# Memory attention and SwiGLU on one core: the first pair's attention taken batch by batch, its root moved ahead of the transposes, PSUM banks named by a table

## The chip, the cores and the metric

The kernel runs on one core of one Trainium2 chip. The metric is device time in microseconds, from one launch that has all inputs in HBM and leaves the output there. Lower is better.

## What is computed

Eight batches of attention with 8 heads, 576 positions, head width 64 and 32 memory slots, and then one RMS-normed SwiGLU layer over the 4608 rows (width 512, inner width 1536), all in float32:

```python
a = softmax(phi, axis=seq)                      # (b, h, 576, 32)
k_m, v_m = a^T @ k, a^T @ v                     # (b, h, 32, 64) each
attn = softmax(q @ k_m^T / 8, axis=slots)       # (b, h, 576, 32)
x = (attn @ v_m) as rows of 512                 # (4608, 512)
xn = x / sqrt(mean(x*x) + 1e-6) * rms_g
out = (silu(xn @ w_gate) * (xn @ w_val)) @ w_out
```

## The kernel before

The batches go in four pairs. For a pair, phi's softmax numerators `e_bd` are multiplied with k and v (`kvp`, line 461), scaled by their sums (`si`, `im`, then `kb` and `vb`, lines 480 to 496) and transposed (`kvt`, copied to `km` and `vt`). Queries are scored against `km`, and a softmax over the 32 slots follows. The product with v_m is never written out for the SwiGLU layer. The scores `at` are scaled by the row's root and split into a high and a low part (`ath`, `atl`), v_m is multiplied into the weight columns (`vp`, `xh` and `xl`), and the gate and value products `pg` and `pv` (line 1069) take those two. The only use of `xp` (scores times v_m, line 845) is its sum of squares, from which the root `rinv` comes (lines 866 to 891). After silu and product, `po` (line 1126) multiplies with w_out and `acc` collects over the inner width. Weights come as float32, are split by bit arithmetic (lines 944 to 989) and are written back to DRAM for the later pairs.

The first pair has its own code, because nothing can hide its beginning. Its queries are loaded into `qs`, a tile for two slices of heads that holds batch 0 in the even and batch 1 in the odd partitions (`load_q`, line 545), so each of the four slices `s` is reordered (`qr`), transposed (`qtp`, copied to `qT`), scored and softmaxed for both batches at once (`q_steps`, `score_steps`). The normed scores stand in `first`. `x_steps(0)` transposes them (`tp`, line 747), copies them to `at`, makes `xp` and the root, and then multiplies `first` with a diagonal matrix of the root (`diag`, line 803, on ScalarE, and `ts`, line 811, on TensorE), so that the transposed and scaled scores come out in one matmul; `ath` (line 830, ScalarE) and `atl` (line 826, VectorE) split them.

The order of all work is written out: `parts` is a list of some 2,790 small steps, and `ISSUE` a table of numbers that says in which order they are put into the program. Each engine runs its own instructions in that order, and so does the SP queue, which issues every DMA. PSUM has two double tiles (`banks`) and four single ones (`bank`), which are handed out in turn:

```python
    def bank(name, shape=None):
        return ps.tile(shape or [P, 512], F32, tag="b", name=name, bufs=4)
```

Of the kernel before, what the change touches and what calls it, by code (L numbers as in the profile page):

```python
# [1230 lines left out]
```

## Time and profile before

| | |
|---|---|
| median of 3 runs | 792.76 us (792.66 to 794.98) |
| the profiled execution | 792.07 us |
| its span, first to last instruction | 790.3 us |
| TensorE (PE) busy | 748.9 us, 95% |
| VectorE (DVE) busy | 471.8 us, 60% |
| ScalarE (ACT) busy | 350.9 us, 44% |
| GpSimd (POOL) busy | 244.4 us, 31% |
| moved by DMA | 112.86 MB |
| mean granted TensorE clock | 0.991 |

Engine times are a union of the spans of its instructions; a share over the whole span mixes a beginning with little matmul work with a long stretch in which TensorE is never free. Idle time of an engine in the tables carries the name of what released it. The profiled execution has 1.8 us outside its span.

### The profile page before, as it was taken

The numbers are of one execution on the slowest core, as the hardware profiler recorded it, in microseconds if no ns is written. First come the engines' busy times: TensorE is split into PE (matmuls) and PEld (weight loads), VectorE is DVE, ScalarE is ACT, GpSimd is POOL, SyncE is SP. The second block draws the span as 40 slices with busy tenths as digits, with TensorE's granted clock in tenths as the row PEclk, the third lists the DMA queues.
The fourth block names the chain that finished last, engine by engine and source line by source line (L and its number), as shares of the span: only waits on it lengthen the run. The fifth ranks groups of instructions, "written<-read, shape, count | busy, mean of one in ns | idle before, by whom it ended". The sixth has DMA issues, their size and how long they took to land.

```text
span 790.3 us, 18128 instructions
## 1 busy us (share of the span) xinstructions
PE 748.9 (95%) x7496; PEld 639.0 (81%) x7496; DVE 471.8 (60%) x956; ACT 350.9 (44%) x697; POOL 244.4 (31%) x209
## 2 busy tenths in 40 slices
PE   4777988999999999999999999899999999999998
PEld 2565766788887988888888888788888888888886
DVE  6698878888776676465565374655454422444443
ACT  1668767665555544532354334442432335232221
POOL 0244555354432223322433212221232212121212
PEclk9799999999999999999999999999999999999999
DMA  9947775856583652253153654222241334112113
GB/s 331 375 148 214 200 184 198 275 177 213 196 216 85 198 152 95 80 174 98 67 181 123 153 170 99 86 81 71 92 134 54 117 110 147 53 56 80 54 54 120
DMA packets 111722, 112.86 MB, mean 143 GB/s; under 512 B 61460, under 2 KB 77848, under 8 KB 111640
## 3 DMA queue, kind: packets, MB, share of 16 engines
q1 hardware_dynamic: 111640, 111.70, 45.2%
q8 instruction: 59, 0.97, 0.5%
q14 instruction: 23, 0.19, 0.1%
HBM read 89.66 MB, written 22.02 MB: 141 GB/s over the span
## 4 chain that ended last, share of the span: by engine, by line
PE 81%; DVE 6%; ACT 5%; DMA 4%; SPq 2%; issue 1%; POOL 0%; ACTq 0%; DVEq 0%
PE po L1126 36%; PE pg L1069 17%; PE pv L1069 17%; PE vp L1034 5%; PE xp L845 2%; SPq L645 2%; DMA kvs<-in_k_dram 1%; PE kvp L461 1%; DMA qs<-in_q_dram 1%; PE S L670 1%; ACT wex L944 1%; DVE phi L407 1%; ACT xh L1051 1%; DMA raw<-in_moe_w_out_dram 1%; ACT L1080 1%
## 5 line engine op out<-in xcount | busy, mean ns | idle before, releaser
L1100 POOL TENSOR_TENSOR hl<-hf,hh 128x512 fp32r<-128x512 f32 (+1 forms) x84 | 120.0, 1431 | 311.8 <-ACT hh L1095 297.9
L1085 DVE TENSOR_TENSOR hf<-pv,sg 128x256 f32<-128x256 f32 (+1 forms) x192 | 85.5, 452 | 153.1 <-PE pv L1069 110.1
L1126 PE MATMUL po<-oh,hh 128*128 128x512 f32 x432 | 172.2, 399 | 2.3 <-ACT acc L1135 1.4
L1080 ACT ACTIVATE sg<-pg 128x256 f32<-128x256 f32 (+1 forms) x192 | 77.6, 411 | 213.9 <-PE pg L1069 183.3
L1137 DVE TENSOR_TENSOR acc<-po,acc 128x512 f32<-128x512 f32 x180 | 121.0, 685 | 84.5 <-PE po L1126 84.0
L1126 PE MATMUL po<-oh,hl 128*128 128x512 f32 x432 | 170.2, 394 | 0.0
L1126 PE MATMUL po<-ol,hh 128*128 128x512 f32 x432 | 169.2, 392 | 0.0
L1095 ACT CAST hh<-hf 128x512 fp32r<-128x512 f32 (+1 forms) x96 | 64.5, 675 | 86.5 <-DVE hf L1085 86.2
L1126 PEld LDWEIGHTS po<-oh,hh 128*128 128x128 f32 x432 | 81.1, 188 | 21.8 <-ACT acc L1135 2.2
L1126 PEld LDWEIGHTS po<-oh,hl 128*128 128x128 f32 x432 | 81.2, 188 | 17.9
L1126 PEld LDWEIGHTS po<-ol,hh 128*128 128x128 f32 x432 | 81.2, 188 | 13.5
L1069 PE MATMUL pv<-ath,xh 128*128 128x320 f32 (+1 forms) x384 | 84.6, 301 | 4.3 <-ACT sg L1080 3.3
L1069 PE MATMUL pg<-ath,xh 128*128 128x256 f32 (+1 forms) x384 | 85.8, 305 | 2.4 <-DVE hf L1085 1.4
L1069 PE MATMUL pv<-ath,xl 128*128 128x320 f32 (+1 forms) x384 | 81.4, 293 | 0.0
L1069 PE MATMUL pg<-ath,xl 128*128 128x256 f32 (+1 forms) x384 | 81.3, 293 | 0.0
L1069 PE MATMUL pg<-atl,xh 128*128 128x256 f32 (+1 forms) x384 | 81.3, 293 | 0.0
L1069 PE MATMUL pv<-atl,xh 128*128 128x320 f32 (+1 forms) x384 | 81.3, 293 | 0.0
L1049 DVE TENSOR_TENSOR xl<-vp,xh 128x512 fp32r<-128x512 f32 x96 | 64.3, 682 | 28.0 <-ACT xh L1051 27.8
L1069 PEld LDWEIGHTS pg<-ath,xh 128*128 128x128 f32 x384 | 62.7, 188 | 16.7 <-issue 5.0
L1069 PEld LDWEIGHTS pv<-ath,xh 128*128 128x128 f32 x384 | 63.4, 188 | 15.3 <-ACT sg L1080 5.3
L1051 ACT CAST xh<-vp 128x512 fp32r<-128x512 f32 x96 | 54.3, 590 | 29.8 <-PE pv L1069 11.7
L1069 PEld LDWEIGHTS pv<-atl,xh 128*128 128x128 f32 x384 | 61.3, 188 | 0.0
(121 smaller groups left out, 998.0 us busy)
## 6 DMA issues: line engine op xcount, KB each, us to landing
wc<-wd SPq DMA_DIRECT2D x36, 512.0 KB, 5.5
oh<-od SPq DMA_DIRECT2D x36, 256.0 KB, 3.6
ol<-od SPq DMA_DIRECT2D x36, 256.0 KB, 3.9
out_dram<-acc SPq DMA_DIRECT2D x36, 256.0 KB, 2.2
q<-in_q_dram SPq DMA_DIRECT2D x96, 72.0 KB, 2.9
raw<-in_moe_w_val_dram SPq DMA_DIRECT2D x12, 512.0 KB, 4.7
raw<-in_moe_w_gate_dram SPq DMA_DIRECT2D x12, 512.0 KB, 4.5
raw<-in_moe_w_out_dram SPq DMA_DIRECT2D x12, 512.0 KB, 4.7
```

Source lines behind the costliest of these rows:

```text
L645: load(d["q", cc][32 * g:32 * g + 32, s], q[b, 4 * cc + 2 * s + h].rearrange("(r x) d -> r x d", r=32)[:, :, 32 * half:32 * half + 32],)
L845: nc.tensor.matmul(xp[64 * j:64 * j + 64, s, t - t0, P * cc:P * cc + P], st["at", pr][rows, t, cc, 64 * j:64 * j + 64], st["kb", 2 * pr + ...
L1034: nc.tensor.matmul(vp[32 * g:32 * g + 32, flip(b, cc), cc, :], vm[pr][rows, b, hp, 32 * (g % 2):32 * (g % 2) + 32], w[rows, hp, :], start= ...
L1049: V.tensor_tensor(out=xl[:, k], in0=src, in1=xh[:, k].bitcast(F32), op=ALU.subtract)
L1051: nc.scalar.copy(xs[i][0][:, k], src)
L1069: nc.tensor.matmul(pt[:, :N], l[:, flip(b, cc), cc, half * P:half * P + P], r[:, b, cc, t0:t0 + n, :].rearrange("p t x -> p (t x)"), start ...
L1080: nc.scalar.activation(sg[:, :N], acts[gi, b, 0][:, :N], AF.Silu)
L1085: V.tensor_tensor(out=acts[gi][:, :, b, :], in0=acts[gi, b, 1][:, :N].rearrange("p (t x) -> p t x", x=64), in1=acts[gi, b, 2][:, :N].rearr ...
L1095: nc.scalar.copy(hh, acts[gi].rearrange("p t b x -> p t (b x)"))
L1100: (V if gi and i < 12 else nc.gpsimd).tensor_tensor(out=hl, in0=acts[gi].rearrange("p t b x -> p t (b x)"), in1=hsplit[i, gi][0].bitcast(F ...
L1126: nc.tensor.matmul(po, l[:, tt, :], r, start=(m == 0), stop=(m == 5))
L1137: V.tensor_tensor(out=accs[key], in0=pt[0], in1=accs[key], op=ALU.add)
```

## The change

Batch 0 and batch 1 of the first pair no longer share tiles. `load_q` puts two head slices of one batch into the lower and upper 64 partitions of its own tile, `q_steps` and `score_steps` take a batch `j`, and `first_steps(j)` replaces what `x_steps(0)` did. The root is now multiplied into `first` on GpSimd (`scaled`) and plain transposes follow (`ts`). Since one batch fills half the rows, the sums of squares come out in two halves, and two small matmuls with a 0/1 matrix `twice` bring them together (`ss`). Squares are 5 instructions for a batch (9 for the pair before), the root 12 VectorE instructions for a batch (12 for each of two parts of the pair before), the diagonal's 9 ScalarE instructions are gone, and `ath`/`atl` take 3 instructions each for a batch (5 for each batch before). PSUM's four single tiles get a tag each, and a string `BANKS` says which one each request takes. `ISSUE` is a new table. Its core:

```diff
     def bank(name, shape=None):
-        return ps.tile(shape or [P, 512], F32, tag="b", name=name, bufs=4)
+        turn[0] += 1
+        return ps.tile(shape or [P, 512], F32, tag="b" + BANK[turn[0] - 1], name=name, bufs=1)
...
-    def load_q(s, j):
-        load(st["q", s][j::2], q[j, 2 * s:2 * s + 2].rearrange("h (p c) d -> p h (c d)", c=NT))
+    def load_q(j, s, half):
+        hp = 2 * half + s
+        load(
+            st["q", j][64 * half:64 * half + 64, s],
+            q[j, 2 * hp:2 * hp + 2].rearrange("h (p c) d -> p h (c d)", c=NT),
+        )
...
+    def first_steps(j):
...
+        def both():
+            d["ss"] = tp = bank(f"ss{j}")
+            for i in range(2):
+                nc.tensor.matmul(
+                    tp[:, i:10 - i:2], st["twice"][:, i].rearrange("p a x -> p (a x)"), st["ssq"][:, j, :5 - i],
+                    start=True, stop=True,
+                )
...
+        def scaled(t0, n):
+            def f():
+                nc.gpsimd.tensor_tensor(
+                    out=st["first"][:, 1, j, t0:t0 + n], in0=st["first"][:, 0, j, t0:t0 + n],
+                    in1=r[:, t0:t0 + n].unsqueeze(2).broadcast_to([P, n, P]), op=ALU.mult,
+                )
+            return f
...
+        steps = []
+        for t0, n in PIECES:
+            steps += [turn(t0, n, 0), copy(t0, n)]
+        for u0 in range(0, 5, 2):
+            steps += [mm(u0)] + [square(x) for x in range(u0, min(u0 + 2, 5))]
+        steps += [both, root]
+        for t0, n in PIECES:
+            steps += [scaled(t0, n), turn(t0, n, 1), put(t0, n, 0), put(t0, n, 1)]
+        return steps
...
-        def scaled(t0):
...
-                    nc.scalar.activation(dg, ident, AF.Copy, scale=rinv[pr][:, t:t + 1])
...
-                        nc.tensor.matmul(
-                            tp[:, o * P:(o + 1) * P], srcs[t][:, cc * P:(cc + 1) * P], d["dg", t],
-                            start=True, stop=True,
-                        )
...
-    for t0, n in GROUPS:
-        for s in range(HP):
-            add(q_steps(s, t0 == 0), score_steps(s, t0, n))
-    add(x_steps(0, lambda t: st["a"][:, t]))
+        for t0, n in GROUPS:
+            for s in range(2):
+                add(q_steps(b, s, t0 == 0), score_steps(b, s, t0, n))
+        add(first_steps(b))
```

What the new table does is seen at three places. In the rows a name carries its batch (`kvs0`, `kvp1`) or its group (`pv0_00`), and a running number behind it.

On the SP queue, near its beginning, stood before:

```order
L334 DMA kvs0_134<-in_k_dram 128x2x576
L334 DMA kvs0_134<-in_v_dram 128x2x576
L334 DMA kvs0_134<-in_k_dram 128x2x576
L334 DMA kvs0_134<-in_v_dram 128x2x576
L334 DMA kvs1_136<-in_k_dram 128x2x576
L334 DMA kvs1_136<-in_v_dram 128x2x576
L334 DMA kvs1_136<-in_k_dram 128x2x576
L334 DMA kvs1_136<-in_v_dram 128x2x576
L546 DMA qs1_137<-in_q_dram 64x2x576
L546 DMA qs0_135<-in_q_dram 64x2x576 x2
L546 DMA qs1_137<-in_q_dram 64x2x576 x2
L546 DMA qs0_135<-in_q_dram 64x2x576 x2
```

and now stands:

```order
L358 DMA kvs0_152<-in_k_dram 128x2x576
L358 DMA kvs0_152<-in_v_dram 128x2x576
L358 DMA kvs0_152<-in_k_dram 128x2x576
L358 DMA kvs0_152<-in_v_dram 128x2x576
L571 DMA qs0_153<-in_q_dram 64x2x576 x4
L1001 DMA raw_00_362<-in_moe_w_gate_dram 128x4x256
L1001 DMA raw_10_450<-in_moe_w_val_dram 128x4x256
L358 DMA kvs1_154<-in_k_dram 128x2x576 x2
L358 DMA kvs1_154<-in_v_dram 128x2x576 x2
L571 DMA qs1_155<-in_q_dram 64x2x576 x4
L349 DMA phi2_621<-in_phi_dram 128x4x288
```

Batch 0's four query loads come ahead of batch 1's k and v, two weight loads between them; batch 1's queries come last. (`qs0` and `qs1` were two head slices of both batches; now they are batch 0 and batch 1.)

On VectorE, between the last products of batch 0's scale and the first of batch 1's (`si1`), stood before:

```order
L434 TENSOR_TENSOR es1_295<-es1_295 128x4x32
L434 TENSOR_TENSOR es1_295<-es1_295,e_bd1_127 128x4x32
L480 TENSOR_SCALAR si1_1_422<-kvp1_298 128x1
L483 RECIPROCAL si1_1_422<-si1_1_422 128x1
L487 TENSOR_TENSOR im1_1_425<-si1_1_422,hmask_107 128x2
L480 TENSOR_SCALAR si1_0_427<-kvp1_298 128x1
L483 RECIPROCAL si1_0_427<-si1_0_427 128x1
L487 TENSOR_TENSOR im1_0_430<-si1_0_427,hmask_107 128x2
L496 TENSOR_TENSOR kb1_436<-kvp1_298,im1_0_430 128x128
L496 TENSOR_TENSOR vb1_446<-kvp1_298,im1_0_430 128x128
L496 TENSOR_TENSOR kb1_436<-kvp1_298,im1_1_425 128x128
```

and now stands:

```order
L458 TENSOR_TENSOR es1_300<-es1_300,e_bd1_128 128x4x32
L636 TENSOR_REDUCE mxs0_0_0_374<-S0_0_0_351 128x8
L640 TENSOR_TENSOR ex0_0_0_376<-S0_0_0_351,mxs0_0_0_374 128x256
L649 TENSOR_REDUCE sm0_0_0_386<-ex0_0_0_376 128x8
L652 TENSOR_SCALAR sm0_0_0_386<-sm0_0_0_386 128x8
L655 RECIPROCAL sm0_0_0_386<-sm0_0_0_386 128x8
L520 TENSOR_TENSOR vb0_397<-kvp0_212,im0_0_322 128x128
L520 TENSOR_TENSOR vb0_397<-kvp0_212,im0_1_317 128x128
L636 TENSOR_REDUCE mxs0_1_0_407<-S0_1_0_365 128x8
...
L1038 SCALAR_TENSOR_TENSOR wex0_0_412<-raw_00_362,wex0_0_412 128x512
L1031 TENSOR_SCALAR wex1_0_452<-wex1_0_452 128x512
L504 TENSOR_SCALAR si1_1_562<-kvp1_480 128x1
```

Between the sums `es1` and batch 1's scale there are now 24 instructions: 17 of the 20 of batch 0's four softmax groups, `vb0`'s two, and five of the first two weight tiles (`wex`).

On TensorE, around the first gate or value product, stood before:

```order
L398 MATMUL mr3_0_1045<-ident_72,mb3_0_1024 128x128
L1034 MATMUL vp1_1047<-wc1_947,vm0_452 32x256 x16
L511 MATMUL kvt2_1014<-ident_72,vb2_997 128x128 x2
L1069 MATMUL pv0_00_1081<-ath0_931,xh0_900 128x256 x2
L1069 MATMUL pv0_00_1081<-atl0_1064,xh0_900 128x256 x2
L1069 MATMUL pv0_00_1081<-ath0_931,xl0_920 128x256 x2
L461 MATMUL kvp3_1091<-kv3_0_922,e_bd1_127 32x128 x2
```

and now stands:

```order
L702 MATMUL xp0_1_4_1040<-vb1_623,at0_462 64x128 x4
L422 MATMUL mr3_0_1054<-ident_72,mb3_0_1034 128x128
L683 MATMUL ts0_0_1057<-ident_72,first_405 128x128 x4
L720 MATMUL ss1_1066<-ssq0_169,twice_163 128x5
L720 MATMUL ss1_1066<-ssq0_169,twice_163 128x4
L683 MATMUL ts0_8_1081<-ident_72,first_405 128x128
L485 MATMUL kvp3_1092<-kv3_0_1048,e_bd1_128 32x128 x2
...
L485 MATMUL kvp3_1092<-e_bd1_128 32x128 x2
L1140 MATMUL pg0_00_1172<-ath0_1062,xh0_842 128x256 x2
L1140 MATMUL pg0_00_1172<-atl0_1170,xh0_842 128x256 x2
L1140 MATMUL pg0_00_1172<-ath0_1062,xl0_849 128x256 x2
L683 MATMUL ts1_0_1195<-ident_72,first_405 128x128 x4
L535 MATMUL kvt2_1205<-ident_72,kb2_1184 128x128 x2
```

The first product is now behind the `kvp` of batch 3 and nearly all of both batches' score work, where it stood ahead of batch 3's `kvp`; batch 2's `kvt` and one `vp` that stood ahead of it come behind it. From about the middle of the program on, TensorE's groups stand in nearly the same order as before.

## Rows read from the trace of the kernel before

**Rows 1.** Windows: stretch, its length, busy of PE, PEld, DVE, ACT, POOL, PE clock, DMA, GB/s

```profile
0.00:26.00 26.00, 11.82 (x313) 8.14 (x313) 13.53 (x50) 4.54 (x6) 0.70 (x6) 0.92 0.96 342
26.00:66.00 40.00, 30.93 (x594) 24.43 (x594) 36.05 (x104) 31.04 (x72) 15.98 (x20) 0.88 0.67 227
66.00:96.00 30.00, 24.14 (x364) 19.71 (x364) 25.22 (x62) 22.83 (x49) 17.26 (x18) 1.00 0.80 207
96.00:160.00 64.00, 58.97 (x565) 46.43 (x565) 53.72 (x101) 43.73 (x85) 27.46 (x20) 1.00 0.73 217
160.00:480.00 320.00, 318.54 (x3233) 275.10 (x3232) 204.10 (x386) 147.70 (x280) 111.71 (x95) 1.00 0.48 147
520.00:790.00 270.00, 266.58 (x2099) 232.83 (x2091) 115.61 (x220) 83.97 (x181) 61.77 (x45) 1.00 0.27 90
```

**Rows 2.** Timeline of VectorE around its two longest gaps after 13 us: start, duration, what, idle before

```profile
17.73 0.16 DVE L480 TENSOR_SCALAR si<-kvp 128x1 f32<-128x1 f32 x1 [2.07 <-PE kvp L471]
...
20.90 0.29 DVE L434 TENSOR_TENSOR es<-es,e_bd 128x128 f32<-128x128 f32 x1
27.96 0.16 DVE L480 TENSOR_SCALAR si<-kvp 128x1 f32<-128x1 f32 x1 [6.77 <-PE kvp L471]
```

**Rows 3.** Timeline of TensorE: the wait behind that gap, and the first value product

```profile
26.92 0.69 PE L511 MATMUL kvt<-ident,vb 128*128 128x128 f32 x2 [2.32 <-ACT km L519]
27.54 0.31 PE L471 MATMUL kvp<-ones,es 64*32 64x1 f32 x16
...
66.51 0.47 PE L1069 MATMUL pv<-ath,xh 128*128 128x256 f32 x2 [0.49 <-DVE phi L407]
```

**Rows 4.** Timeline of ScalarE in the same stretch

```profile
25.87 0.72 ACT L553 COPY qr<-qs 128x640 f32<-128x640 f32 x1 [1.59 <-DMA qs<-in_q_dram]
26.50 0.37 ACT L519 COPY km<-kvt 128x256 f32<-128x256 f32 x1
```

**Rows 5.** Groups by form, VectorE: count, busy us, mean ns, idle before

```profile
L967 DVE SCALAR_TENSOR_TENSOR wex<-raw,wex 128x512 int32<-128x512 int32 x36 | 24.7, 688 | 0.5
...
L599 DVE TENSOR_REDUCE mxs<-S 128x8 f32<-128x256 f32 x4 | 1.7, 418 | 0.1
...
L618 DVE RECIPROCAL sm<-sm 128x8 f32<-128x8 f32 x4 | 0.8, 203 | 0.1
```

**Rows 6.** Groups by form, TensorE: the products with the diagonal, and the plain transposes

```profile
L811 PE MATMUL ts<-first 128*128 128x128 f32 x36 | 6.0, 320 | 5.4 <-ACT first L803 5.4
...
L747 PE MATMUL tp<-ident,first 128*128 128x128 f32 x18 | 3.3, 325 | 0.6 <-DVE ex L603 0.6
```

**Rows 7.** Windows of line 461 alone: batch 3's `kvp`, busy of PE, of PEld, clock, DMA

```profile
67.50:71.00 3.50, 2.57 (x144) 2.15 (x144) 1.00 0.78 287
```

**Rows 8.** Timeline of TensorE, 57 to 66 us

```profile
59.95 1.10 PE L845 MATMUL xp<-vb,at 64*64 64x128 f32 x32
...
64.56 1.09 PE L1034 MATMUL vp<-wc,vm 64*32 64x256 f32 x32
```

**Rows 9.** Timelines of VectorE and of GpSimd, 44 to 49 us

```profile
44.07 0.42 DVE L948 TENSOR_SCALAR wex<-wex 128x512 f32<-128x512 f32 x1
...
47.92 0.90 DVE L948 TENSOR_SCALAR wex<-wex 128x512 f32<-128x512 f32 x1
...
47.13 1.41 POOL L624 TENSOR_TENSOR first<-ex,sm 128x320 f32<-128x320 f32 x2 [0.42 <-DVE sm L615]
48.49 0.63 POOL L434 TENSOR_TENSOR es<-es 128x128 f32<-128x128 f32 x1
```

**Rows 10.** DMA issues, 8 to 28 us: count, KB each, us to landing

```profile
qs<-in_q_dram SPq DMA_DIRECT2D x8, 288.0 KB, 10.2
```

**Rows 11.** Timeline of the SP queue, 70 to 86 us

```profile
71.07 3.11 SPq L645 DMA_DIRECT2D q<-in_q_dram  x4
...
84.70 0.56 SPq L927 DMA_DIRECT2D raw<-in_moe_w_out_dram  x1
```

**Rows 12.** Groups by form: the addition that empties a `po` bank

```profile
L1137 DVE TENSOR_TENSOR acc<-po,acc 128x512 f32<-128x512 f32 x180 | 121.0, 685 | 84.5 <-PE po L1126 84.0
```

More of the change, by code (lines that the diff above doesn't have):

```diff
@@ L280 @@
         bank(f"b{i}_first")
+    for tag, n in (
+        ("acc0", 1), ("acc1", 1), ("hf0", 1), ("mc", 4), ("mxp", 2), ("sg", 2), ("xh", 2), ("si", 2), ("im", 2),
+        ("hh0", 3), ("hl1", 3), ("hl0", 3), ("hh1", 3), ("xl", 2), ("mxs", 2), ("sm", 2), ("hf1", 1),
+    ):
+        sb.tile([P, 1], F32, tag=tag, name=f"{tag}_first", bufs=n)
     load = nc.sync.dma_start
@@ L541, in kv_steps, with twice, q_steps @@
         )
-    def load_q(s, j):
-        load(st["q", s][j::2], q[j, 2 * s:2 * s + 2].rearrange("h (p c) d -> p h (c d)", c=NT))
-    def q_steps(s, first):
+    def load_q(j, s, half):
[4 more added lines that the diff above has]
+        )
+    def twice():
+        st["twice"] = tw = sb.tile([P, 2, 2, 64], F32, tag="hl0", name="twice", bufs=3)
+        nc.gpsimd.memset(tw, 0.0)
+        for i in range(2):
+            rows = slice(64 * i, 64 * i + 64)
+            for a in range(2):
+                nc.gpsimd.tensor_copy(tw[rows, i, a], ident[rows, rows])
+        st["ssq"] = persist.tile([P, 2, 5], F32, tag="ssq0", name="ssq0")
+        nc.gpsimd.memset(st["ssq"], 0.0)
+    def q_steps(j, s, first):
         g0, gn = GROUPS[0 if first else 1]
         def order():
-            st["qr", s, g0] = qr = small(0, [P, gn, 2, 64], "qr", f"qr0_{s}_{g0}")
+            st["qr", j, s, g0] = qr = small(0, [P, gn, 2, 64], "qr", f"qr{j}_{s}_{g0}")
             nc.scalar.copy(
                 qr.rearrange("p c h d -> p h c d"),
-                st["q", s].rearrange("p h (c d) -> p h c d", c=NT)[:, :, g0:g0 + gn],
+                st["q", j][:, s].rearrange("p h (c d) -> p h c d", c=NT)[:, :, g0:g0 + gn],
             )
@@ L562, in f @@
                 if t0 < 8:
-                    st["qT", s, t0] = small(0, [P, 4 if first else 5, P], "qT", f"qT0_{s}_{t0}")
-                qr = st["qr", s, g0]
-                st["qtp", s, t0] = tp = bank(f"qtp0_{s}_{t0}")
+                    st["qT", j, s, t0] = small(0, [P, 4 if first else 5, P], "qT", f"qT{j}_{s}_{t0}")
+                qr = st["qr", j, s, g0]
+                st["qtp", j, s, t0] = tp = bank(f"qtp{j}_{s}_{t0}")
                 for t in range(t0, t0 + n):
@@ L579, in q_steps, with score_steps @@
         return [order] + (turn(0) if first else turn(4) + turn(8))
-    def score_steps(s, t0, n):
+    def score_steps(j, s, t0, n):
         d = {}
         def mm():
-            qT = st["qT", s, t0]
-            sp = bank(f"S0_{s}_{t0}")
+            qT = st["qT", j, s, t0]
+            sp = bank(f"S{j}_{s}_{t0}")
             for t in range(n):
-                for j in range(2):
+                for half in range(2):
+                    rows = slice(64 * half, 64 * half + 64)
                     nc.tensor.matmul(
-                        sp[64 * j:64 * j + 64, 64 * t:64 * t + 64],
-                        qT[:, t, j::2],
-                        st["km", j][:, s, :],
+                        sp[rows, 64 * t:64 * t + 64], qT[:, t, rows], st["km", j][:, 2 * half + s, :],
                         start=True, stop=True,
@@ L610, in total @@
         def total():
-            d["sm"] = small(0, [P, 2 * n, 1], "sm", f"sm0_{s}_{t0}")
+            d["sm"] = small(0, [P, 2 * n, 1], "sm", f"sm{j}_{s}_{t0}")
             V.tensor_reduce(out=d["sm"], in_=d["ex"], axis=AX.X, op=ALU.add)
@@ L630, in score_steps, with turn, copy, f @@
         return [mm, [top, sub], exp, [total, chain([guard, invert]), norm]]
+    def first_steps(j):
+        d = {}
+        own = slice(64 * j, 64 * j + 64)
+        r = rinv[0] if j == 0 else tiny[:, :NT]
+        ri = r.bitcast(I32)
+        m, u = (tiny[:, 10 * x:10 * x + NT] for x in (1 + 2 * j, 2 + 2 * j))
+        def turn(t0, n, low):
+            def f():
+                if "at" not in st:
+                    st["at"] = st["at", 0] = persist.tile([P, NT, 2, P], F32, tag="at", name="at0")
+                d[low, t0] = tp = bank(f"{('tp', 'ts')[low]}{j}_{t0}")
+                for t in range(t0, t0 + n):
+                    nc.tensor.transpose(
+                        out=tp[:, (t - t0) * P:(t - t0 + 1) * P], in_=st["first"][:, low, j, t], identity=ident,
+                    )
+            return f
+        def copy(t0, n):
+            def f():
+                (V.tensor_copy if t0 == 4 else nc.scalar.copy)(
+                    st["at"][:, t0:t0 + n, :, own], d[0, t0][:, :n * P].rearrange("p (t c x) -> p t c x", c=2, x=64),
+                )
+            return f
+        def mm(u0):
+            def f():
+                d["xp", u0] = xp = banks(f"xp0_{j}_{u0}")
+                for t in range(2 * u0, min(2 * u0 + 4, NT)):
+                    for cc in range(2):
+                        for s in range(2):
+                            rows = slice(64 * s, 64 * s + 64)
+                            nc.tensor.matmul(
+                                xp[64 * (t % 2):64 * (t % 2) + 64, s, t // 2 - u0, P * cc:P * cc + P],
+                                st["at"][rows, t, cc, own],
+                                st["kb", j, 1][rows, cc].rearrange("p h d -> p (h d)"),
+                                start=True, stop=True,
+                            )
+            return f
+        def square(x):
+            def f():
+                n = P if x < 4 else 64
+                xp = d["xp", x & ~1][:n, :, x % 2]
+                nc.scalar.activation(xp, xp, AF.Square, accum_out=st["ssq"][:n, j, x:x + 1])
+            return f
+        def both():
+            d["ss"] = tp = bank(f"ss{j}")
+            for i in range(2):
+                nc.tensor.matmul(
+                    tp[:, i:10 - i:2], st["twice"][:, i].rearrange("p a x -> p (a x)"), st["ssq"][:, j, :5 - i],
+                    start=True, stop=True,
+                )
+        def root():
+            V.tensor_scalar(
+                out=m, in0=d["ss"][:, :NT], scalar1=1.0 / DM, scalar2=1e-6, op0=ALU.mult, op1=ALU.add
+            )
+            V.tensor_scalar(out=m, in0=m, scalar1=1e-6, scalar2=-0.5, op0=ALU.max, op1=ALU.mult)
+            V.tensor_scalar(
+                out=ri, in0=m.bitcast(I32), scalar1=-0.5, scalar2=float(0x5F3759DF - (1 << 22) - (1 << 30)),
+                op0=ALU.mult, op1=ALU.add,
+            )
+            for a in range(3):
+                V.tensor_tensor(out=u, in0=r, in1=r, op=ALU.mult)
+                V.tensor_tensor(out=u, in0=u, in1=m, op=ALU.mult)
+                V.scalar_tensor_tensor(out=r, in0=u, scalar=1.5, in1=r, op0=ALU.add, op1=ALU.mult)
+        def scaled(t0, n):
+            def f():
+                nc.gpsimd.tensor_tensor(
+                    out=st["first"][:, 1, j, t0:t0 + n], in0=st["first"][:, 0, j, t0:t0 + n],
+                    in1=r[:, t0:t0 + n].unsqueeze(2).broadcast_to([P, n, P]), op=ALU.mult,
+                )
+            return f
+        def put(t0, n, low):
+            def f():
+                key, held = (("ath0", at_hi), ("atl0", at_lo))[low]
+                if 0 not in held:
+                    held[0] = persist.tile([P, 2, 2, NT, 64], F32R, tag=key, name=f"{key[:3]}0")
+                src = d[1, t0][:, :n * P].rearrange("p (t c x) -> p c t x", c=2, x=64)
+                hi = at_hi[0][:, j, :, t0:t0 + n, :]
+                if low:
+                    V.tensor_tensor(
+                        out=at_lo[0][:, j, :, t0:t0 + n, :], in0=src, in1=hi.bitcast(F32), op=ALU.subtract
+                    )
+                else:
+                    nc.scalar.copy(hi, src)
+            return f
+        steps = []
[7 more added lines that the diff above has]
+        return steps
@@ L727, in attend_steps, with x_steps @@
         )
[L731 to L733 removed]
+    def x_steps(pr):
+        tps, xps = {}, {}
         i = pr % 2
[L736 to L760 removed]
         def spread(t0, n):
@@ L894, in newton @@
                 return [g0, g1, g2]
-            steps = [f0, f1, f2] + [newton(a) for a in range(3)]
-            return chain(steps) if pr == 0 else steps
+            return [f0, f1, f2] + [newton(a) for a in range(3)]
         steps = []
         for t in range(NT):
-            if not pr and t % 2 == 0:
-                steps += [turn(t), copy(t)]
             if t % 2 == 0:
@@ L906, in x_steps @@
         steps.append(fin(4, NT))
-        if pr == 0:
-            return steps + [scaled(t0) for t0 in range(0, NT, 2)]
         for t0, n in PIECES:
```

97 lines of the change are left out of this document (26 added, 71 removed), and 303 rows, old and new, of the table ISSUE.

## The prediction, made before the changed kernel ran

> **What bounds the kernel now.** The table of windows comes first, because a share over the whole span hides that this program has two parts. From 160 us on TensorE is busy for 318.54 of 320 us, and for 266.58 of the last 270 [rows 1]: that stretch is made of matmuls and can only be moved to the left. Before 160 us TensorE is free for 14.2 us of the first 26, 9.1 of the next 40, 5.9 of the next 30 and 5.0 of the next 64, some 34 us in all. In 26 to 66 us VectorE is busy for 36.05 of 40 us, more than any other engine [rows 1]. So the beginning is paced by VectorE, once it has something to do, and the question is what it has to do in the first 26 us, where it is busy for 13.53.
>
> The timeline of VectorE shows its longest gap. Batch 0's work ends at 21.2 us, and the next instruction starts at 27.96, after 6.77 us of waiting for `kvp` [rows 2]. That product was not late by its data. TensorE stood before it at a transpose (`kvt`) that waited 2.32 us for ScalarE's copy `km` [rows 3], and ScalarE had put `km` behind a copy of the queries, which waited for their load until 25.87 us [rows 4]. The queries of both batches were loaded last, behind the k and v of both. So VectorE idled 6.77 us for the last load. The first gate or value product starts at 66.51 us [rows 3].
>
> **What the change does to it.** Batch 0's queries now land ahead of batch 1's k and v. In the first 26 us 342 GB/s were moved [rows 1], 8.9 MB with the start-up in it. Phi, k and v of batch 0 and its queries are 4.7 MB, at that mean rate 14 us; with batch 1's k and v and the weights between it is 8.1 MB, 24 us, and with batch 1's queries 9.3 MB, 27 us. These are estimates. Batch 0 can therefore be scored from about 19 us on, after one reorder, transpose, copy and product, while batch 1's data still come.
>
> *VectorE.* The order puts 24 instructions into the gap: 17 of softmax, two of `vb0`, five of weights. A reduction over 256 columns takes 418 ns, a weight step up to 688, a small one 203 [rows 5]. With eleven wide softmax steps at 0.42 to 0.48, six small ones at 0.2, two products at 0.28 and five weight steps at 0.53 the sum is about 9 us by duration; neighbours overlap by about a fifth, so it is some 7 us of VectorE's time. The 0.48, 0.28 and 0.53 are estimates from these rows by width. The number of VectorE instructions ahead of the first gate or value product is about the same in both programs (140 rows against 140), so what goes into the gap comes out of the paced stretch. Bounds: 0 where the gap isn't filled, 6.77 us where it is, and 2.07 more where the smaller gap ahead of 17.73 us goes too [rows 2]. I take 6.0, near the gap's own length, less the waits for the exponentials, which alternate between the engines. The first product then starts at about 60.5 us. Late next: batch 1's queries, at 27 us.
>
> *TensorE behind the first product.* It now has less left. Ahead of that product come batch 3's `kvp`, 2.57 us [rows 7], eight more `xp` products, half of the 1.10 us that 16 take [rows 8], two more transposes, and 13 plain `ts` transposes where eight matmuls with the diagonal stood. One `vp`, 1.09 us [rows 8], and four `kvt` transposes go behind it. A matmul with the diagonal is two records, 36 records for 18 of them with 6.0 us busy, where 18 plain transposes are 3.3 us [rows 6]: 0.33 against 0.18 us each. So 2.57 + 0.55 + 0.37 + (13 x 0.18 - 8 x 0.33) - 1.09 - 4 x 0.18 = 1.4 us more is done by then. In all, 18 x 0.15 = 2.7 us is gone and four small `ss` products come, 0.1 us each by the nearest small ones. What is left behind is 1.4 + 2.3 = 3.7 us less, and since TensorE sets the pace from there, I count all of it. Bounds: 2 where the free time of 66 to 160 us absorbs the first part, 3.7 at most.
>
> *GpSimd and ScalarE.* GpSimd gets six multiplications of `first` by the root and loses nothing. It is busy 15.98 of 40 us [rows 1], so its own time is covered. But it can hold VectorE up: `wex` took 0.42 us beside an idle GpSimd and 0.90 across two of GpSimd's instructions [rows 9]. Six such meetings would cost 2.9 us, none nothing; the multiplications meet many reductions and PSUM readers too, so I take 0.5. ScalarE loses nine diagonals, four `ath` and gains a square and a copy; it is not the pace, so nothing is counted, and TensorE's 5.4 us of waiting for diagonals [rows 6] is part of the free time, not of the sum. The `twice` matrix and the zeroed `ssq` are made while GpSimd has nothing else. The dummy tiles cost no instruction.
>
> *The sum.* 792.07 - 6.0 - 3.7 + 0.5 = 782.9 for an execution like the profiled one. That one ran 0.7 us under the median of the three, so the median comes to **783.6 us**.
>
> **The rivals.**
>
> *The queries land late all the same.* Eight query loads of 288 KB took 10.2 us each to land among the others [rows 10]. They went to every second partition; now each goes to 64 adjoining ones. At the 342 GB/s of the mean a batch's 1.18 MB take 3.4 us; at half of it 3.4 more, which delays batch 0's scores by 3.4 us and batch 1's by 6.9. Of the gap 3.4 us stays open, and other weight and phi steps cover most of the rest: about 4 us, 787.6. The transfers of before say nothing on adjoining halves, so the price is only an estimate. The Trainium skill (SBUF — State Buffer, section Door 1: The DMA port swizzle) says that a transfer into 64 partitions of one half reaches only half of the ports, and that two such transfers mostly serialize; no run here shows it yet, it speaks against this change, and by it alone the time would be this rival's 787.6. Chance 0.20.
>
> *The gap is not filled*, because batch 0's chain from load to softmax goes to and fro between three engines and no two groups overlap, or the change's order doesn't start it early. Then only the 3.7 us of TensorE's remain: 789.6. Chance 0.08.
>
> *More is gained.* Batch 3's `kvp` frees the tiles for the next pair's queries: the SP queue starts them at 71.07 us, right behind it, and only at 84.70 does it come to the third of w_out [rows 11]. Now that `kvp` stands ahead of the first product, so this moves by some 10 us rather than 6. If half of TensorE's free 10.9 us between 66 and 160 [rows 1] goes with it, the time is 778.2. Chance 0.16.
>
> *Slower, by the banks.* A request for a PSUM bank took the next in turn; now the table names one. Where it names a bank that was just filled, TensorE waits for the addition that empties it, 685 ns [rows 12]. The program has 216 `po` groups. At 17 such waits (11.6 us) the change is slower by over 0.3%, at 25 it takes 800.7. Against it: the table and the order belong together, and the last half of the order is nearly the old one, which has almost no free time [rows 1]. Chance 0.09.
>
> **How the numbers follow.** The sum above has 0.42, the rivals 0.53, and mixtures that come out even 0.05. I take 0.3%, 2.4 us, as what a measurement here can tell from no change: faster is below 790.4. Faster are the sum, the late queries, the gain in the later stretch and half of the unfilled gap: 0.42 + 0.20 + 0.16 + 0.04 = 0.82. The same: the other half of that and the mixtures, 0.09. Slower: 0.09. The range goes from 774, beyond the rival with more gain, to 790, the unfilled gap; about 0.06 lies below it and 0.12 above.
>
> **What would show it.** Right: VectorE's longest gap in 16 to 28 us is under 2.5 us; the first gate or value product starts at 58 to 63 us; TensorE's busy time falls by 2 to 3 us; from 160 us on the windows look as before. The late queries would show as a batch 0 whose first reorder starts after 18 us and as a batch 1 that starts after 32. A wrong prediction would show as a first product after 66 us, or as TensorE waiting for `acc` in the windows behind 160 us.

## The result: 803.2 us, slower by 1.25%, against a forecast of 783.6

| | before | changed |
|---|---|---|
| median, us (four runs each, same chip) | 793.76 | 803.22 |
| range | 792.66 to 794.98 | 801.80 to 806.74 |
| ratio, 95% interval | | 1.0125, 1.0084 to 1.0167 |
| profiled execution: time, span | 792.07, 790.3 | 801.8, 800.0 |

The windows of the changed kernel, columns as in [rows 1]:

```profile
0.00:26.00 26.00, 11.99 (x221) 9.11 (x221) 15.88 (x57) 8.90 (x14) 2.35 (x13) 1.00 0.96 292
26.00:66.00 40.00, 28.35 (x599) 22.32 (x598) 27.25 (x78) 23.35 (x53) 17.26 (x22) 0.79 0.72 215
66.00:96.00 30.00, 22.37 (x357) 17.82 (x365) 24.30 (x63) 16.45 (x36) 14.95 (x17) 0.94 0.84 208
96.00:160.00 64.00, 57.14 (x576) 46.14 (x561) 56.93 (x109) 45.43 (x87) 26.70 (x19) 0.97 0.65 195
160.00:480.00 320.00, 315.25 (x3252) 273.24 (x3259) 207.86 (x383) 144.53 (x277) 114.76 (x99) 1.00 0.51 153
```

Three things differ from [rows 1]. The first 26 us moved 292 GB/s, not 342. VectorE does 2.4 us more there and 8.8 us less in 26 to 66. TensorE is free for 40.2 us before 160 us, against 34.1, and was granted 0.79 of its clock in 26 to 66. Added up over windows of 1 us, it stood at half clock (1.2 GHz) for 23.9 us of the first 200, against 13.7.

Finer windows of the changed kernel show when the rate fell:

```profile
12.00:16.00 4.00, 2.10 (x51) 1.49 (x58) 3.21 (x7) 1.17 (x1) 0.00 (x0) 1.00 1.06 224
16.00:20.00 4.00, 4.00 (x128) 3.74 (x110) 1.80 (x7) 1.47 (x3) 0.00 (x0) 1.00 1.07 233
20.00:24.00 4.00, 2.78 (x42) 1.96 (x40) 2.37 (x12) 2.74 (x7) 0.00 (x0) 1.00 1.07 376
28.00:32.00 4.00, 2.78 (x38) 2.06 (x36) 2.93 (x9) 2.04 (x4) 0.67 (x2) 0.70 1.07 217
32.00:36.00 4.00, 2.32 (x151) 2.04 (x152) 1.94 (x5) 0.47 (x1) 0.67 (x1) 1.00 1.04 263
```

The same windows of the kernel before:

```profile
16.00:20.00 4.00, 2.58 (x113) 2.15 (x101) 2.10 (x11) 0.00 (x0) 0.00 (x0) 1.00 1.05 390
28.00:32.00 4.00, 3.75 (x18) 2.95 (x19) 3.66 (x15) 3.87 (x9) 0.65 (x1) 0.50 1.07 387
```

The DMA engines are busy throughout in both (next to last column), but in the two stretches in which the changed kernel loads queries they move 217 to 263 GB/s instead of 390. Against 390 the four slow windows lack 1.7, 1.6, 1.8 and 1.3 us of transfers, 6.4 us in all: the loads beside the queries are slowed with them. Its timelines of ScalarE, VectorE and TensorE show what came late:

```profile
16.92 1.24 ACT L591 COPY qr<-qs 128x640 f32<-128x640 f32 x2 [1.32 <-DMA qs<-in_q_dram]
...
23.07 0.42 DVE L636 TENSOR_REDUCE mxs<-S 128x8 f32<-128x256 f32 x1 [1.38 <-PE S L628]
36.38 0.16 DVE L504 TENSOR_SCALAR si<-kvp 128x1 f32<-128x1 f32 x1 [1.79 <-PE kvp L495]
43.91 0.69 DVE L690 COPY at<-tp 128x512 f32<-128x512 f32 x1 [2.21 <-PE tp L683]
...
32.65 0.62 PE L485 MATMUL kvp<-kvs,e_bd 64*32 64x128 f32 x25 [1.87 <-DMA kvs<-in_v_dram]
75.30 0.50 PE L1140 MATMUL pg<-ath,xh 128*128 128x256 f32 x2
```

VectorE's gap of 6.77 us [rows 2] is gone, and up to 80 us none over 2.3 us is left. But batch 1's k and v land at 32.65, 8.6 us after the estimate, and the first gate or value product starts at 75.30, not at 60.5 as forecast and not at 66.51 as before [rows 3]. Of the two signs of late queries one came: batch 1's first reorder starts at 37.90, behind the 32 us named, but batch 0's at 16.92, ahead of the 18. The sign of costly banks didn't come: behind 160 us the longest wait of TensorE for `acc` is this one (total, times, longest):

```profile
PE pg L1140 <- DVE acc L1208: 0.2, 1, 0.2
```

### The profile page after: what moved, and what is told of

Same layout as the page of the kernel before. It is cut to its first block, busy times and chain, and to the rows that moved or that the text cites. A ratio compares the mean times of both kernels' runs of the same rounds, so it can differ in the third digit from the quotient of the medians.

```text
span 800.0 us, 18082 instructions
## 1 busy us (share of the span) xinstructions
PE 750.3 (94%) x7486; PEld 642.9 (80%) x7486; DVE 476.3 (60%) x952; ACT 347.6 (43%) x687; POOL 251.1 (31%) x221
## 4 chain that ended last, share of the span: by engine, by line
PE 80%; DMA 7%; DVE 4%; ACT 4%; issue 2%; SPq 1%; DVEq 0%; ACTq 0%
PE po L1197 34%; PE pv L1140 17%; PE pg L1140 17%; PE vp L1105 5%; PE kvp L485 2%; DMA kvs<-in_v_dram 2%; DMA raw<-in_moe_w_out_dram 2%; PE xp L921 2%; DMA qs<-in_q_dram 1%; PE xp L702 1%; DMA q<-in_q_dram 1%; DMA raw<-in_moe_w_gate_dram 1%; DMA ol<-od 1%; ACT xp L714 1%; SPq L784 1%
## 5 line engine op out<-in xcount | busy, mean ns | idle before, releaser
L1140 PEld LDWEIGHTS pv<-ath,xh 128*128 128x128 f32 x384 | 64.0, 189 | 12.5 <-issue 4.2
```

The costliest lines, as they stand in the source:

```text
L1140: nc.tensor.matmul(pt[:, :N], l[:, flip(b, cc), cc, half * P:half * P + P], r[:, b, cc, t0:t0 + n, :].rearrange("p t x -> p (t x)"), start ...
```

## The experiments

Ratios are against runs of the kernel before on the same chip, with 95% intervals.

### The layout of the queries, both ways and alone

*e1_spread*, the changed kernel without the adjoining halves:

```diff
-            st["q", j][64 * half:64 * half + 64, s],
+            st["q", j][half::2, s],
-                        sp[rows, 64 * t:64 * t + 64], qT[:, t, rows], ...
+                        sp[rows, 64 * t:64 * t + 64], qT[:, t, half::2], ...
```

> The changed kernel with one thing undone: each query load goes to every second partition again (as in the kernel before) and not to 64 adjoining ones; order, root, banks as changed. Theory 1 (the adjoining halves make the loads slow, and the late data cost the time): the rate in 8 to 40 us no longer falls to 173 to 250 GB/s and stays near 390; kvs1 lands before 28 us (32.65 in the changed kernel), the first gate or value product starts at 62 to 68 us (75.30), the time is 784 to 795 us. Rival (the new order itself is late: the to and fro of batch 0, the weight loads moved behind it): the first product stays behind 72 us and the time within 799 to 806.

Measured: 796.23 us, ratio 1.0026 (1.0005 to 1.0047). Its windows and its first product:

```profile
16.00:20.00 4.00, 2.94 (x91) 2.30 (x72) 3.25 (x15) 2.61 (x7) 0.00 (x0) 1.00 1.09 367
28.00:32.00 4.00, 2.62 (x160) 2.35 (x146) 3.20 (x12) 0.69 (x2) 0.72 (x1) 1.00 1.01 335
...
0.00:26.00 26.00, 12.01 (x261) 9.25 (x261) 17.11 (x62) 10.75 (x20) 2.49 (x13) 1.00 0.96 338
26.00:66.00 40.00, 27.15 (x641) 20.77 (x637) 32.94 (x92) 25.69 (x58) 18.74 (x22) 0.93 0.75 242
66.00:96.00 30.00, 23.76 (x346) 18.46 (x347) 24.26 (x56) 16.81 (x35) 15.62 (x17) 0.87 0.75 177
96.00:160.00 64.00, 58.75 (x556) 49.05 (x555) 56.43 (x112) 44.98 (x87) 27.03 (x20) 1.00 0.67 203
...
70.38 0.59 PE L1140 MATMUL pg<-ath,xh 128*128 128x256 f32 x2
```

The rate is back, and 7.6 us with it: the changed kernel is 9.5 us above the kernel before on its chip (803.22 against 793.76), this one 1.8 us on its own (796.23 against 794.4). The first product lies between the two theories, the time 1.2 us above the range of the first: with the layout undone the new order still gives nothing. The profiled execution, 793.16 us, is one of the shorter.

*e2_adjoining*, the kernel before with the layout alone:

```diff
-        load(st["q", s][j::2], ...
+        load(st["q", s][64 * j:64 * j + 64], ...
-                        qT[:, t, j::2],
+                        qT[:, t, 64 * j:64 * j + 64],
```

> The kernel before with one thing added: each query load goes to 64 adjoining partitions; order and all else as before. Theory 1 (adjoining halves are slow loads): the rate falls below 260 GB/s where the queries of the first pair land, the wait of VectorE for kvp grows from 6.77 to 11 us or more, and the time rises by 4 to 8 us, to 797 to 802. Rival (the layout costs nothing, the order does): the rate stays near 390 and the time within 2.4 us of the kernel before.

Measured: 800.92 us against 794.4, ratio 1.0089 (1.0059 to 1.0119). Window and VectorE's wait:

```profile
24.00:28.00 4.00, 3.26 (x90) 2.65 (x90) 0.00 (x0) 0.00 (x0) 0.00 (x0) 0.50 1.05 210
...
36.13 0.16 DVE L480 TENSOR_SCALAR si<-kvp 128x1 f32<-128x1 f32 x1 [14.74 <-PE kvp L471]
```

6.5 us one way, 7.6 the other: the layout's price is shown.

*e7_loads_alone* replaces the program by eight stages of loads.

> Loads alone; the kernel computes nothing else and leaves the output unwritten but for a corner. Eight stages of 2.36 MB, each begun when the one ahead has landed: A eight loads of 288 KB into every second partition, B the same into 64 adjoining partitions, the two halves in turn, C the same, four loads into the first half and then four into the second, D four loads of 576 KB into all 128 partitions; then A to D again. Theory 1 (64 adjoining partitions are slow whatever else runs): A and D take about 6 to 8 us with their latency, at 390 GB/s, B and C 10 to 14 us. Rival (only the mixture with other loads or the alternation is slow): B or C is as fast as A.

VectorE's timeline, where each stage's wait is the brackets' number (B, C, D, then A, B, C):

```profile
23.71 0.18 DVE L47 COPY t2C<-t1B 128x8 f32<-128x8 f32 x1 [12.20 <-DMA t1B<-in_q_dram]
37.24 0.17 DVE L47 COPY t3D<-t2C 128x8 f32<-128x8 f32 x1 [13.35 <-DMA t2C<-in_q_dram]
46.37 0.17 DVE L47 COPY t4A<-t3D 128x8 f32<-128x8 f32 x1 [8.95 <-DMA t3D<-in_k_dram]
57.23 0.17 DVE L47 COPY t5B<-t4A 128x8 f32<-128x8 f32 x1 [10.69 <-DMA t4A<-in_q_dram]
70.06 0.17 DVE L47 COPY t6C<-t5B 128x8 f32<-128x8 f32 x1 [12.65 <-DMA t5B<-in_q_dram]
83.64 0.17 DVE L47 COPY t7D<-t6C 128x8 f32<-128x8 f32 x1 [13.41 <-DMA t6C<-in_q_dram]
```

A took 10.7 us, B 12.2 and 12.7, C 13.4 twice, D 9.0. The order is as expected, but A and D missed their 6 to 8 us, and the distance is smaller: the eight issues of A take the SP queue 5.2 of its 10.7 us, and in no window of 2 us does A fill the DMA engines (0.94 at most). In 2 us windows B and C stay at 256 GB/s or below, and D reaches 406. Putting the halves in turn (B) wins 7% over one after the other (C). The Trainium skill (SBUF — State Buffer, section "Can I just issue two DMAs to hit both halves?") measured two such transfers at once at 6% above one; the trace agrees (12.4 us for B on average, 13.4 for C).

### The banks

*e3_banks_in_turn*, the changed kernel with `tag="b", bufs=4` where it had `tag="b" + BANK[turn[0] - 1], bufs=1`.

> The changed kernel with the four PSUM banks given in turn instead of by the table of names. Theory 1 (the loads cost the time, the banks nothing): within 3 us of the changed kernel, 800 to 806. Rival (the named banks make TensorE wait): at least 4 us faster than the changed kernel, below 798.

Measured: 810.22 us, ratio 1.0200 (1.0174 to 1.0225), some 6 us slower than the changed kernel when each is set against the kernel before on its chip. Neither theory said this: the named banks don't cost. That they save is not shown. The first product starts at 82.60, 7.3 us later, and ahead of it the trace names no wait for a bank. What differs is a longer wait that no other engine ends (1.04 us in the changed kernel) and 41.0 us at half clock against 23.9:

```profile
36.35 1.96 PE L485 MATMUL kvp<-kvs,e_bd 64*32 64x128 f32 x64 [2.75 <-issue]
```

### The root

*e4_root_only* and *e14_gap_root* (the same on top of e5, below):

```diff
-                    nc.scalar.activation(dg, ident, AF.Copy, scale=rinv[pr][:, t:t + 1])
+                    nc.scalar.activation(srcs[t], srcs[t], AF.Copy, scale=rinv[pr][:, t:t + 1])
-                        nc.tensor.matmul(tp[...], srcs[t][...], d["dg", t], start=True, stop=True)
+                        nc.tensor.transpose(out=tp[...], in_=srcs[t][...], identity=ident)
```

> The kernel before with the root alone put on ahead: ScalarE multiplies each of the nine 128x256 pieces of first by its root where it made a diagonal matrix, and plain transposes stand where matmuls with the diagonal stood. Theory (what the prediction said of this part): TensorE's busy time falls by 18 x 0.15 = 2.7 us, ScalarE's grows by about 1 us, and the time falls by 2 to 3 us against the kernel before. Rival (the diagonal matmuls lay beside waits, or fewer TensorE columns lower its clock): within 1 us of before or slower.

> e5_gap_closed and e4_root_only together: the gap shortened by order, and the root put on ahead of plain transposes, nothing filled. If the parts add by TensorE's work: 2 to 3 us below e5_gap_closed, 789 to 791. If e4_root_only's longer half clock (27.3 us against 13.7) and its waits come here too: 793 to 798.

Measured: e4 797.47 us, ratio 1.0033 (1.0010 to 1.0056); e14 794.45, ratio 0.9995 (0.9976 to 1.0013), where e5 alone has 0.9971. The 2.7 us of matmuls that are left out buy nothing, twice. (Here ScalarE multiplies by the root, in the changed kernel GpSimd; that form wasn't run alone.) In e4's profiled execution, one of its longer (798.96 us), the first product is no earlier (67.58 against 66.51), and behind it TensorE waits 3.03 us, where the kernel before waits 0.78 at the same product, for a silu on ScalarE behind a weight step whose tile was late:

```profile
124.25 0.66 ACT L942 ACTIVATE wex<-raw 128x512 f32<-128x512 f32 x1 [2.14 <-DMA raw<-in_moe_w_out_dram]
...
126.41 0.50 PE L1067 MATMUL pv<-ath,xh 128*128 128x256 f32 x2 [3.03 <-ACT sg L1078]
```

### Is VectorE the pace?

*e5_gap_closed* moves rows of the order of the kernel before:

```diff
-    55, 95, 54, 29, 223, 30, 127, 62, 57, 56, 275, 58, 63, 753, 96, 67, 64, 85, ...
+    55, 57, 95, 54, 29, 223, 30, 127, 62, 63, 275, 56, 58, 67, 64, 85, 96, 65, ...
```

> The kernel before with its gap of 6.77 us shortened by order alone: ScalarE's copy km of batch 0 stands ahead of the query copies, the sums of kvp for batch 1 ahead of the transposes kvt, and two query copies ahead of the weight step; loads and all else as before. Theory 1 (VectorE paces what follows, so time taken out of its gap is gained): its first instruction of batch 1 starts at 25.0 us instead of 27.96, the first score at 29 to 30 instead of 31.9, and the time falls by 2 to 3 us. Theory 2 (what paces is the data, the to and fro of the engines and TensorE's clock): the gap shrinks and the time stays within 1 us of before.

Measured: 792.59 us, ratio 0.9971 (0.9953 to 0.9989). VectorE and the first product:

```profile
25.70 0.16 DVE L476 TENSOR_SCALAR si<-kvp 128x1 f32<-128x1 f32 x1 [3.54 <-PE kvp L467]
28.93 0.43 DVE L944 TENSOR_SCALAR wex<-wex 128x512 f32<-128x512 f32 x1 [1.42 <-ACT wex L940]
31.32 0.43 DVE L944 TENSOR_SCALAR wex<-wex 128x512 f32<-128x512 f32 x1 [0.70 <-ACT wex L940]
...
66.86 0.48 PE L1065 MATMUL pv<-ath,xh 128*128 128x256 f32 x2 [0.50 <-DVE phi L403]
```

The gap shrank by 3.2 us, and 2.1 us of it came back at once as waits for weights. The median fell by 2.1 us, as the first theory said (2 to 3 us). In this execution, one of the longer (793.64 us), the first product didn't move (66.51 before). *e20_gap_silu* (below) has the same order up to that product; in its profiled execution, one of the shorter (790.19 us), it starts 2.2 us earlier than before:

```profile
64.30 0.48 PE L1065 MATMUL pv<-ath,xh 128*128 128x256 f32 x2 [0.45 <-DVE phi L403]
```

So closing the gap by order alone is worth some 2 us. No kernel with the whole computation was faster: e5 and e20 beat both kernels, by 0.2 to 0.3%.

*e15_before_less_vector* and *e16_spread_less_vector* leave out the same twelve steps of VectorE:

```diff
+            if (kind, n) in LEFT_OUT:
+                return
             V.tensor_scalar(
```

> The kernel before with twelve VectorE steps left out (the clamp and the shift of the first six weight tiles, so that these weights are not converted rightly): in the kernel before they take 6.3 us between 29 and 65 us, where VectorE is busy 36 of 40 us. Nothing else changes. Theory 1 (VectorE paces this stretch, as the prediction said): the first gate or value product starts 4 to 6 us earlier than 66.5 and the time falls by 3 to 6 us. Theory 2 (TensorE's waits there are a to and fro between the engines, in which a busy VectorE is not the last to end): the first product moves by under 2 us and the time falls by less than 1.5 us.

> e1_spread (the changed kernel with the queries in every second partition) with the same twelve VectorE steps left out, about 5 us between 27 and 62 us, where VectorE is busy 33 of 40 us. Theory 1 (VectorE still paces): the first product starts 3 to 5 us earlier than 70.4 and the time falls by 3 to 5 us. Theory 2 (the chain of each batch from engine to engine paces): under 2 us and under 1.5 us.

Measured: e15 791.45 us, ratio 0.9970 (0.9952 to 0.9989); e16 797.08, ratio 1.0034 (1.0017 to 1.0051). With 6.3 us less of VectorE's work the kernel before starts its first product 2.6 us earlier, at 63.90, and is 2.4 us faster. That is between the theories. In the profiled execution (793.41 us, two over the median) the start was lost again at a late tile:

```profile
121.46 0.66 ACT L946 ACTIVATE wex<-raw 128x512 f32<-128x512 f32 x1 [2.10 <-DMA raw<-in_moe_w_out_dram]
...
123.62 0.50 PE L1075 MATMUL pv<-ath,xh 128*128 128x256 f32 x2 [3.00 <-ACT sg L1086]
```

In e16 the first product starts where it does in e1_spread (70.34 against 70.38), and the time didn't fall. But this execution is one of the longer (799.88 us): batch 0's v came late, and batch 1's first score starts at 38.54, in e1_spread at 36.82. From that score to the first product, e16 and then e1_spread (columns as in [rows 1]):

```profile
14.25 3.85 PE L487 MATMUL kvp<-kvs,e_bd 64*32 64x128 f32 x132 [0.70 <-DMA kvs<-in_v_dram]
...
38.54:70.34 31.80, 23.95 (x566) 18.37 (x566) 23.96 (x73) 20.57 (x46) 17.65 (x22) 0.89 0.64 217
36.82:70.38 33.56, 25.07 (x565) 19.64 (x566) 26.82 (x80) 20.36 (x46) 19.39 (x24) 0.85 0.68 217
```

With 2.9 us less of VectorE's work that way is 1.8 us shorter. In e15 the way from the first score (31.60, before 31.90) is 2.3 us shorter with 3.5 us less (29.44 against 32.96). So VectorE is a part of the pace in both orders, some 0.6 us for each of its own there, as far as single executions can tell. Why e16's time didn't fall stays open; it holds another cost, 5.3 us of issue idle (waits that no other engine ends) against 2.2 in e1_spread, 2.2 of them at 446.21.

*e17_less_vector_silu*, *e18_gap_root_silu* and e20 move unit 1206, the silu in that wait, ahead of 861, the weight step.

> e15_before_less_vector (twelve VectorE weight steps left out) with one ScalarE instruction moved: the silu of pg that TensorE waited 3.0 us for at 123.6 us stands ahead of the weight step that waited for the late w_out tile, not behind it. Theory 1 (the 2.7 us gained by then were lost at this wait and at the half clock behind it, 124 to 131 us): that wait is under 1 us, the second output step starts at 170 to 171.5 us instead of 173.6, and the time is 2 to 3 us below e15, 788 to 790. Theory 2 (another wait takes its place): within 1 us of e15.

> e14_gap_root with the same silu moved ahead of the weight step. In e14's profiled run the weight step waited 0.7 us there, in e4_root_only's 2.1. Theory 1 (a start that is earlier only reaches the end if ScalarE's queue lets the silu pass the late tile): 1 to 3 us below e14, 791.5 to 793.5 against its 794.45. Theory 2: within 1 us of e14.

> e5_gap_closed with the same silu moved; the candidate for the fastest. Theory 1: as e5 or up to 1.5 us faster, 791 to 792.6, since e5's first product is no earlier than that of the kernel before and the tile was in time there. Theory 2 (the moved weight step is late in its turn): slower than 793.5.

Measured: 793.05 us (0.9988, 0.9971 to 1.0004), 795.78 (1.0026, 1.0010 to 1.0043) and 792.26 (0.9979, 0.9962 to 0.9995): e17 is no better than e15, e18 some 2 us worse than e14 by the ratios, e20 as e5. In e17 the wait changed its name at the same place:

```profile
123.77 0.64 PE L1071 MATMUL pg<-ath,xh 128*128 128x256 f32 x2 [2.53 <-DVE hf L1087]
```

### The lower clock, and filled waits

All five add transposes of the identity into a tile that the next real matmul overwrites:

```diff
+    def warm(to, n):
+        for _ in range(n):
+            nc.tensor.transpose(out=to, in_=ident, identity=ident)
...
+            warm(sp[:, :P], 5 * j)
```

> The changed kernel with the queries in every second partition, and 42 transposes of the identity added, which nobody reads, at places of batch 1 to 3 where TensorE waited (five ahead of each of four scores, four ahead of xp and of ss, nine and five ahead of the kvp of batches 2 and 3). They are 42 x 0.165 = 6.9 us of TensorE at the full clock. Theory A (a lower granted clock costs e1_spread its gain): the clock stays at 1.00 in 44 to 72 us, where e1_spread shows 0.50 to 0.88, kvp of batches 2 and 3 takes 2.6 us each instead of 4.1 and 5.0, and the time is 2 to 5 us below e1_spread. Theory B (the chain sets it, whatever the clock): within 1.5 us of e1_spread, or slower by up to 3 us.

> The changed kernel with 47 transposes of the identity added, which nobody reads, at places where TensorE waited for data there: eleven ahead of the kvp of batch 1, seven ahead of its first qtp, five ahead of each of its scores, four ahead of its xp and of its ss, five ahead of the kvp of batch 3. They are 7.8 us at the full clock. Theory A (the late queries cost the time twice, by the wait and by the lower clock that TensorE is granted after a wait): the time at half clock falls from the 23.9 us of the changed kernel to 8 to 16 us and the time by 3 to 6 us, to 797 to 801. Theory B (the wait alone costs): the same as the changed kernel or up to 4 us slower.

> e5_gap_closed with 51 such transposes where TensorE waited for data: eight ahead of the kvp of batch 1, seven and five ahead of two qtp, sixteen, three and twelve ahead of the first three ts. They are 8.4 us at the full clock. Theory A: the time at half clock, 13.6 us in e5_gap_closed, falls under 6 us and the time by 2 to 5 us, to 788 to 791, below both kernels. Theory B: the time stays within 1.5 us of e5_gap_closed, 791 to 794, or is longer.

> e9_gap_closed_filled with the root put on ahead, as in e4_root_only (which had 27.3 us at half clock and came out 2.6 us slower than the kernel before). Theory A (e4_root_only lost to the clock what it saved in matmuls): with the waits filled the clock holds, and the time is 2 to 3 us below e9_gap_closed_filled, 785 to 789. Theory B (the root's part saves nothing on the path): within 1 us of e9_gap_closed_filled.

> e5_gap_closed with the 51 added transposes all at the very beginning, ahead of TensorE's first work, where it has nothing to do for 11 us (51 x 0.165 = 8.4 us); no wait is filled, and every later TensorE instruction stands 51 places, each of two instructions, later in the instruction stream. Theory 1 (the 7.2 us of 'issue' idle of e9_gap_closed_filled, 1.2 in e5_gap_closed, come from where instructions stand in the stream): issue idle of 4 us or more, among it the 1.7 us near 445 us, and 795 to 799 us. Theory 2 (they come from the transposes standing in the waits, or the fills delay what is behind them): issue idle within 1 us of e5_gap_closed's and 791 to 794 us.

| | us | ratio, interval | at half clock, us | issue idle, us |
|---|---|---|---|---|
| e6 (e1_spread: 796.23, 13.7, 2.2) | 794.79 | 1.0013, 0.9995 to 1.0030 | 10.2 | 3.7 |
| e8 (changed: 803.22, 23.9, 1.8) | 804.77 | 1.0128, 1.0093 to 1.0163 | 6.8 | 7.1 |
| e9 (e5: 792.59, 13.6, 1.2) | 797.69 | 1.0044, 1.0024 to 1.0063 | 3.4 | 7.2 |
| e10 (e14: 794.45, 13.6, 3.1) | 795.54 | 1.0017, 1.0000 to 1.0033 | 10.2 | 1.9 |
| e13 (e5) | 799.60 | 1.0070, 1.0046 to 1.0093 | 23.9 | 7.6 |

Half clock is summed from 1 us windows up to 200 us, issue idle from TensorE's timeline. In e8 the clock is full throughout 26 to 66 us (0.79 in the changed kernel), and the time doesn't fall:

```profile
26.00:66.00 40.00, 26.93 (x649) 21.68 (x651) 29.22 (x80) 23.48 (x53) 17.60 (x22) 1.00 0.79 231
```

Theory A fell in e8 and e9. e6 lies 1.4 us below e1_spread and e10 2.2 below e9, with no gain over the kernel before, and e10 has 5.3 us less of issue idle than e9, so its distance isn't the root's. e9 has 6.0 us more of idle time that no other engine ends, as much as its span is longer than e5's (797.9 against 791.8). TensorE's waits of e9:

```profile
PE qtp L569 <- issue: 3.1, 1, 3.1
PE kvp L462 <- issue: 2.9, 3, 1.7
PE tp L749 <- issue: 1.2, 1, 1.2
```

e13 fills no wait and has the same idle time, among it 2.0 us at 445.7 where e9 has 1.7 at 445.3; its 799.60 us lie just above the 795 to 799 of the first theory. So this cost hangs on where an instruction stands in the stream, not on what it does. What the clock alone costs stays open: every filled kernel also moved the stream.

## Why the prediction was wrong, step by step

**Where the time went.** 7.6 of the 9.5 us are the adjoining halves, to which the sum gave nothing. The rest, order, root and banks together, is 1.8 us over the kernel before, where the sum said 9.2 less. So two steps failed.

**The queries land late all the same.** This rival had the mechanism. Its delay, "at half of it 3.4 more, which delays batch 0's scores by 3.4 us and batch 1's by 6.9", came close to the transfers that are lacking, 3.3 us in the first slow stretch and 3.1 in the second. That is in part luck: the rate didn't fall to half of 342 GB/s, but the loads beside the queries were slowed too. The first scores are 2.2 and 4.9 us later than in e1_spread (22.33 against 20.13, 41.70 against 36.82). The step that failed is what followed: "of the gap 3.4 us stays open, and other weight and phi steps cover most of the rest: about 4 us". Nothing covered it. The first product is 4.9 us later than in e1_spread, as much as batch 1's first score, and in e2_adjoining 8.4 later than before (74.94 against 66.51), since batch 1's k and v and all that is queued behind the queries were late with them; at the end it is 6.5 to 7.6 us. The Trainium skill (SBUF — State Buffer, section Door 1: The DMA port swizzle) spoke against the change, and e1, e2 and e7 bear it out (217 to 263 GB/s against 390 in the windows above). That two such transfers serialize stands in the section named with e7, not in this one. No row spoke against the rule, so 0.20 was too little.

**VectorE: 6.0 us.** This failed whatever the layout: "So what goes into the gap comes out of the paced stretch". Up to the first product, before and in e1_spread:

```profile
0.00:66.51 66.51, 42.77 (x907) 32.60 (x908) 50.09 (x155) 35.69 (x78) 17.20 (x27) 0.90 0.79 273
0.00:70.38 70.38, 43.27 (x1034) 33.78 (x1035) 53.60 (x168) 37.28 (x79) 25.17 (x41) 0.93 0.83 277
```

In e1_spread the gap is filled, and in the first 26 us VectorE is idle for 8.9 us instead of 12.5. But up to the first product it is idle for 16.8 us against 16.4, so as much came up again behind 26 us, and it has 3.5 us more to do by then. I had counted "140 rows against 140"; the traces have 168 instructions and 155 (both roots stand ahead of the product in e1_spread). So nothing came out, and the product is 3.9 us later. That VectorE paces was half right: in e5, e15 and e16 a part of the time taken from it came back, not all. What has to be filled is TensorE's free time, and that grew: 38.3 us before 160 us (26 - 12.01, 40 - 27.15, 30 - 23.76, 64 - 58.75) against 34.1. In the first 26 us TensorE did 12.01 us of work against 11.82: with batch 0 scored early it waits there for VectorE and ScalarE where it waited for loads.

**TensorE behind the first product: 3.7 us.** From that product to the end e1_spread takes 721.0 us and the kernel before 723.8, but that execution of e1_spread is 3.1 us under its median, and the changed kernel takes 724.7 (800.0 - 75.30). So this gain isn't shown. Ahead of the product TensorE did 0.5 us more (43.27 against 42.77) and not 1.4, and in e4 and e14 the root's 2.7 us alone brought no time.

**GpSimd: 0.5 us.** No run tested it, and its row was misread: the step of 0.42 us at 44.07 [rows 9] was not beside an idle GpSimd, which began an `es` sum at 44.23.

**Slower by the banks** fell: 0.2 us of waits, and e3 is some 6 us slower without the table.

**Not settled:** which wait absorbs an earlier start in e4, e14 and e15. e17 removed the one that the trace named, and another of 2.5 us took its place within 0.2 us.

## What to carry to other kernels

Before crediting an order with a gap that it fills, ask whose free time ends the program: here TensorE's, and the filled gap of VectorE didn't reduce it. Add up the work and the idle time of the engine up to a marker (the first product), in both orders: here both grew. A change of layout in a load that stands ahead of everything is charged to all that is queued behind it, so price it at the marker, not at the gap that it was meant for. Such a layout can be tried alone in the old kernel: e2 changed two lines.
